# A conformer block on one core: token tiles of 128 rows in place of 127

## The chip, the cores and the metric

The kernel runs on one core of one Trainium2 chip. A core has five engines that run side by side, each with its own queue of instructions: TensorE (PE; its weight loads are listed as PEld), VectorE (DVE), ScalarE (ACT), GpSimd (POOL) and SyncE (SP, which here issues nearly all DMAs). The metric is the device time of one execution in microseconds, the median of three runs.

## What is computed

A conformer block on x of 2 batches x 4000 tokens x 512 features, bfloat16:

```python
h  = silu(layernorm(x) @ w_ff1_a) @ w_ff1_b          # 512 -> 2048 -> 512
x1 = x + 0.5 * h
h  = layernorm(x1)
p  = softmax((h @ w_q) @ (h @ w_k).T * 512**-0.5)    # 4000 x 4000 per batch
x2 = x1 + (p @ (h @ w_v)) @ w_o
a, b = split(layernorm(x2) @ w_pw1)
dc = depthwise_conv3(a * sigmoid(b))                 # 3 taps along the tokens
x3 = x2 + silu(batchnorm(dc)) @ w_pw2
x4 = x3 + 0.5 * (silu(layernorm(x3) @ w_ff2_a) @ w_ff2_b)
out = layernorm(x4)
```

4000 is neither a multiple of 127 nor of 128: 31 x 127 + 63, or 31 x 128 + 32.

## The kernel before

**Tiles and chunks.** Tokens lie on the partitions in tiles of `TILE` = 127 rows (line 16); four tiles make a chunk of `CHUNK` = 508 (line 18). A batch has `TCB` = 8 chunks, seven of 508 and one of 444 (`width`, line 40): three whole tiles and a rest of `TAIL` = 63 rows. The rests of both batches share one tile (`SHARED`), batch 1 from row `HALF` = 64 on (`tile_rows`, line 54), so the 16 chunks hold 63 tiles, and the last chunk of all has three. Half a chunk is `HC` = 254.

**Feed-forward 1** (`ff1`, line 2572) goes through the 16 chunks. In each, 16 blocks of 128 hidden features are made from the transposed, normalised tokens `lnT`, in which every tile has 128 columns per feature group, of which `0:TILE` are read: the moving operand of the first product is 4 pieces of 127 columns (`ff_first`, line 1200), or 2 pieces in the fast chunks, where `ff_quad` (line 1359) forms products of halves so that seven stand for eight. The second product (`ff_units`, line 1244, seven for eight as well) has `TILE` tokens as its weights (stationary) and 256 columns of `Wb` as moving operand. `ff_plain` and `ff_last` do the last chunk, with 381 columns.

**Attention** (`attention`, line 1969). Per chunk of queries, scores against 31 key tiles of 128 and a rest of 32 keys. `q_group` (line 1565) makes the queries `qT`, whose four rows of a partition are `CHUNK` elements long and lie end to end (line 687). The first chunk of a batch multiplies plainly (`scores`, line 1659, moving operand `qT[:, cc, 0:W]`); the other seven do quads of key tiles by seven products of half width (`score_quad`, line 1912), on parts of `qT` and on differences of them, `QF` (line 672). Exponentials go to the buffers `T`, `R` and sums of them `F` (lines 591 to 596, rows of `HC`), which `pv` (line 1757) multiplies with the values, again with seven products for eight. In a quad, product 5 goes to bank h and ACT copies it away; product 1 goes to another bank and ACT copies it into h; product 6 adds to h; DVE's `plus` reads h; only then product 7 may write h.

**Convolution, feed-forward 2.** The pointwise product, gate and taps run beside attention for 13 chunks and after it for the last ones (from line 2682); `G` holds a chunk and a token on either side, in rows of `GW` = 512 elements (line 716). `swish` (line 2439) makes `z`, then feed-forward 2 goes like 1. At the change of stage the weights are loaded in eight slices; `clear` (line 2754) says how many may be loaded ahead of the last convolution work, since the buffers of that work lie in the same place.

**Moves.** A move of token rows goes in two DMAs, rows 0 to 111 and 112 to 126 (`ROWS`, line 532): to and from the copy `xd` in memory (`put_x`, `get_x`), inputs and outputs and the stored keys (`pieces`, line 1004), and the very first tiles (`load_rows`, line 990), where SP issues the first piece and, for two of the four tiles, ACT the second, in the same queue as the first weights.

**Order.** Every operation is first collected and then laid out by `Plan` (line 110): from an estimate of each duration, which depends on the number of elements, it fixes the order of the instructions on each engine. `ff1`, `attention` and the rest only give the order in which operations are offered, how far one may be taken ahead, and the dependences through buffers.

Of the kernel before, what the change touches and what calls it, by code (L numbers as in the profile page):

```python
# [5 lines left out]
F32 = mybir.dt.float32  # L6
# [6 lines left out]
B, T, D, F, KW = 2, 4000, 512, 2048, 3  # L13


TILE = 127
TPC = 4
CHUNK = TPC * TILE
N = B * T
TCB = -(-T // CHUNK)  # L20
FC = F // 128
NCK = B * TCB
TAIL = T % TILE
NT = NCK * TPC - 1
SHARED = TCB * TPC - 1
HALF = 64
PAIRS = 15
GROUPS = 8
QUADS = 7
# [3 lines left out]
DC = D // 128  # L33
# [6 lines left out]
def width(c):  # L40

    return CHUNK if c % TCB < TCB - 1 else T - (TCB - 1) * CHUNK
# [11 lines left out]
def tile_rows(c, ti):  # L54

    if c % TCB < TCB - 1 or ti < TPC - 1:
        return slice(0, TILE)
    lo = c // TCB * HALF
    return slice(lo, lo + TAIL)
# [466 lines left out]
class Conformer:  # L526
# [2 lines left out]
    TAIL_AT = 22  # L529
    NP = 8  # L530

    ROWS = ((0, 112), (112, TILE))

    NBESIDE = 13

# [22 lines left out]
    def memory(self):  # L558
# [5 lines left out]
        self.place(TCB - 1, self.SLOTS)  # L564
        self.xd = nc.dram_tensor("xd", [NCK, TILE, TPC * D], BF16, kind="Internal").ap()
        self.b_xd = [Buf("xd%d" % c) for c in range(NCK)]

        E = Region(nc, "sums", 35840)
# [36 lines left out]
        A = Region(nc, "keys", 65536)  # L605
# [21 lines left out]
        W = Region(nc, "wff", 32768)  # L627
# [11 lines left out]
        def take(n):  # L639
# [6 lines left out]
                    for s in range(2)]  # L646
# [1 line left out]
                      for s in range(2)]  # L648

        self.lins = [[C.view(oLT + s * 4096, DC * n).rearrange("p (c k) -> p c k", c=DC) for s in range(2)]  # L650
                     for n in (512, 448)]
        self.lin = self.lins[0][1]
        oLM = take(4096)
        self.ltm = [C.view(oLM + j * 1024, D) for j in range(TPC)]
# [58 lines left out]
        self.b_ptail = W.buf("ptail", 31744, 2 * CHUNK)  # L713
        self.pqd = nc.dram_tensor("pqd", [128, TILE], BF16, kind="Internal").ap()
        self.b_pqd = Buf("pqd")
        GW = CHUNK + 4
        self.vst, self.b_vst = W.view(28672, 2 * D), W.buf("vst", 28672, 4 * D)
        self.vs2, self.b_vs2 = W.view(30720, 2 * HD), W.buf("vs2", 30720, 4 * HD)
        self.vs1, self.b_vs1 = C.view(oP + 7680, HD), C.buf("vs1", oP + 7680, 2 * HD)
# [4 lines left out]
        self.b_asb = [W.buf("asb", 8192 + k * 2048, 4 * CHUNK) for k in range(3)]  # L724
        self.tmp = W.view(12288, CHUNK, F32)
        self.b_tmp = W.buf("tmp", 12288, 4 * CHUNK)
        self.bst = W.view(14848, DC * NCK * 6, F32).rearrange("p (c t s) -> p c t s", c=DC, t=NCK)
        self.b_bst = [W.buf("bst", 14848 + cc * NCK * 24, NCK * 24) for cc in range(DC)]
        gof = [16384, 20480]
        self.G = [W.view(o, DC * GW).rearrange("p (c k) -> p c k", c=DC) for o in gof]  # L730
        self.b_G = [[W.buf("G", o + cc * 2 * GW, 2 * GW) for cc in range(DC)] for o in gof]
        self.b_Gl = [[Buf("Gl") for cc in range(DC)] for o in gof]
# [41 lines left out]
            st.units = []  # L774
            self.ff.append(st)

        self.two = A.view(65536 - 256, 128)
        self.b_two = A.buf("two", 65536 - 256, 256)

        ns = self.LN_SLOTS  # L780

# [222 lines left out]
    def pieces(self, c, flat, tiles, lo=0, hi=TPC):  # L1004
# [8 lines left out]
        if last:  # L1013
            for b in range(B):
                e = (b + 1) * T
                res.append((flat[e - TAIL:e, :], tiles[b * HALF:b * HALF + TAIL, TPC - 1, :]))
        return res
# [558 lines left out]
    def queries(self, qc, sl):  # L1576

        last = qc == TCB - 1
        return self.lins[last][sl], T - width(qc) - (T - 448) if last else 0

    def fetch_queries(self, b, qc, ti):
        if ti:
# [856 lines left out]
    def swish(self, t, cc):  # L2439
        z, W = self.z[t % 2][:, cc, :], width(t)  # L2440
        parts = [(z[:, 0:W], t, 0, W)]
        if t == TCB - 1:

            parts.append((z[:, W:CHUNK], NCK - 1, 2 * W - CHUNK, W))
        for out, u, lo, hi in parts:
            self.act(out, self.dcv[u][cc][:, lo:hi], AF.Silu,
                     [self.b_dcv[u][cc], self.b_rsc[cc], self.b_shc[cc]], [self.b_z[t % 2][cc]],
                     bias=self.shc[:, cc:cc + 1], scale=self.rsc[:, cc:cc + 1])
# [52 lines left out]
    def constants(self):  # L2501
        S = self.S
        S.op("POOL", lambda e: e.memset(self.neghalf, -0.5), writes=[self.b_neghalf])
        S.op("DVE", lambda e: e.memset(self.zero, 0.0), writes=[self.b_zero])
        for sl in range(self.LN_SLOTS):
            S.op("DVE", lambda e, sl=sl: e.memset(self.st[sl][:, :, 6:8], 0.0), writes=self.b_st[sl])
            S.op("DVE", lambda e, sl=sl: e.memset(self.st[sl][:, :, 8:9], D * EPS), writes=self.b_st[sl])
        for j in range(TPC):
            S.op("DVE", lambda e, j=j: e.memset(self.ltm[j], 0.0), writes=[self.b_ltm[j]])
        S.op("POOL", lambda e: e.memset(self.onef, 1.0), writes=[self.b_onef])  # L2510
        S.op("POOL", lambda e: e.memset(self.eps2, 2 * EPS), writes=[self.b_eps2])
        S.op("DVE", lambda e: e.memset(self.XT[SHARED][HALF - 32:HALF], 0.0), writes=[self.bx[SHARED]])
        S.op("POOL", lambda e: e.memset(self.ident, 0.0), writes=[self.b_ident])
        S.op("POOL", lambda e: e.affine_select(
            out=self.ident, in_=self.ident, pattern=[[-1, 128]], compare_op=ALU.not_equal, fill=1.0,
            base=0, channel_multiplier=1), reads=[self.b_ident], writes=[self.b_ident])
        S.op("POOL", lambda e: e.memset(self.onec, 1.0), writes=[self.b_onec])
        S.op("POOL", lambda e: e.memset(self.one3, 1.0), writes=[self.b_one3])


    def program(self, any_score):
        i = self.i
        self.any_score = any_score
        S = self.S
# [135 lines left out]
        last = NCK - 1  # L2660
# [90 lines left out]
        self.swish(0, 0)  # L2751
        self.swish(0, 1)
        copy_away()
        clear = (14848 - 12288) // (F // self.NWA * 2)
        for k in range(clear):
            self.load_wa(i["w_ff2_a"], k)
        all_t = range(TPC)
# [145 lines left out]
```

## Time and profile before

| what | us |
|---|---|
| median of three runs | 1890.38 (1889.82 to 1892.54) |
| the profiled execution | 1891.78 |
| its span, first to last instruction | 1887.7 |
| PE busy | 1864.2 |
| PEld busy | 1503.1 |
| DVE busy | 1575.4 |
| ACT busy | 1181.0 |
| POOL busy | 133.3 |

Stages by time in the span: feed-forward 1 up to about 400 us, attention to 1412, the change of stage to 1444, feed-forward 2 to the end. Busy times overlap, since the engines run at once. All work stands under line 93, a helper that records every operation, so groups of instructions are told apart by the tiles that they write and read (`y<-work,keys`: into bank y, from the regions work and keys) and by shape: `128*127 128x256` is a matmul with weights of 128 rows and 127 columns and 256 moving columns. `keys`, `sums`, `work`, `wff` and `xt` are the five memory regions, `s` and `y` the eight accumulator banks.

### The profile page before, as it was taken

The page shows a single profiled execution, that of the slowest core. Times are in us where ns is not written, and L with a number is a line of the kernel's source. Part 1 is how long each engine was busy: PE and PEld are TensorE (multiplying, and loading weights), DVE is VectorE, ACT ScalarE, POOL GpSimd, SP SyncE. Part 2 cuts the span into 40 slices and gives each one's busy share as a digit, 9 for nine tenths or more (in the row PEclk, how much of TensorE's full clock was granted, in tenths as well). Part 3 has the DMA queues.
Part 4 walks back from the last instruction along what each step waited for, and adds up shares of the span by engine and source line. Part 5 has one row for each costly group of instructions (what it writes and reads, how often), then busy time and mean ns, then how long its engine had stood idle before and what let it go on. Part 6 is the DMA issues. An engine that isn't in the chain of part 4 may idle for free.

```text
span 1887.7 us, 38980 instructions
## 1 busy us (share of the span) xinstructions
PE 1864.2 (99%) x15362; PEld 1503.1 (80%) x15362; DVE 1575.4 (83%) x3315; ACT 1181.0 (63%) x2061; POOL 133.3 (7%) x235
## 2 busy tenths in 40 slices
PE   9999999999999999999999999999998999999998
PEld 5899999966777777777677777777774999899897
DVE  7788888868779888888888788879887888888875
ACT  5777777644555665565446555655557777777773
POOL 1000000000000000000000000000011000000000
PEclk9999999999999999999999999999999999999999
DMA  8333344297655665447954544454376322322121
GB/s 187 97 85 90 79 112 105 57 259 218 175 145 140 161 189 150 109 134 172 241 128 126 140 120 111 129 137 120 107 208 169 77 57 68 78 46 62 49 43 33
DMA packets 333646, 231.82 MB, mean 123 GB/s; under 512 B 208264, under 2 KB 305867, under 8 KB 333199
## 3 DMA queue, kind: packets, MB, share of 16 engines
q1 hardware_dynamic: 332777, 228.91, 46.7%
q8 instruction: 123, 2.02, 0.5%
q14 instruction: 68, 0.56, 0.1%
q10 hardware_dynamic: 678, 0.34, 0.1%
HBM read 128.30 MB, written 55.65 MB: 97 GB/s over the span
## 4 chain that ended last, share of the span: by engine, by line
PE 93%; DVE 3%; ACT 1%; DMA 1%; issue 0%; SPq 0%; POOL 0%; ACTq 0%; DVEq 0%
PE s L93 47%; PE y L93 46%; DVE work L93 2%; ACT work L93 1%; DMA work<-work 1%; DVE sums L93 1%; DVE xt L93 0%; DVE s L93 0%; DMA wff<-keysd 0%; ACT sums L93 0%; DVE wff L93 0%; SPq L93 0%; DMA xt<-in_x_dram 0%; POOL work L93 0%; ACT xt L93 0%
## 5 line engine op out<-in xcount | busy, mean ns | idle before, releaser
L93 ACT ACTIVATE sums<-s 128x508 bf16<-128x508 f32 (+2 forms) x494 | 288.8, 585 | 262.7 <-PE s L93 261.4
L93 ACT ACTIVATE keys<-s 128x508 bf16<-128x508 f32 (+1 forms) x281 | 164.1, 586 | 189.1 <-PE s L93 168.8
L93 PE MATMUL y<-work,keys 128*127 128x256 bf16 x1920 | 244.7, 273 | 0.0
L93 DVE TENSOR_TENSOR sums<-sums 128x508 bf16<-128x508 bf16 (+4 forms) x528 | 195.2, 398 | 47.3 <-ACT sums L93 43.0
L93 PE MATMUL s<-work,keys 128*128 128x254 bf16 (+5 forms) x1456 | 224.6, 291 | 0.8 <-ACT sums L93 0.6
L93 PEld LDWEIGHTS y<-work,keys 128*127 128x127 bf16 x1920 | 216.2, 137 | 5.1
L93 PE MATMUL y<-wff,keys 128*127 128x256 bf16 (+3 forms) x1592 | 209.1, 276 | 1.1 <-DVE keys L93 0.9
L93 DVE BATCH_NORM_STATS2 work<-xt 127x6 f32<-127x512 bf16 x311 | 204.9, 681 | 5.4 <-DMA xt<-in_x_dram 4.1
L93 PE MATMUL y<-sums,keys 128*128 128x254 bf16 (+1 forms) x1440 | 201.5, 269 | 0.0
L93 PE MATMUL s<-sums 128*128 128x254 bf16 x1296 | 194.3, 273 | 0.0
L93 PEld LDWEIGHTS y<-wff,keys 128*127 128x127 bf16 (+1 forms) x1592 | 176.0, 136 | 15.1 <-issue 3.3
L93 DVE TENSOR_TENSOR keys<-keys 128x1016 bf16<-128x1016 bf16 (+2 forms) x262 | 168.2, 660 | 22.1 <-ACT keys L93 14.1
L93 PE MATMUL y<-work,wff 128*128 128x254 bf16 (+2 forms) x1116 | 184.0, 292 | 0.0
L93 POOL TENSOR_TENSOR work<-work 127x4 f32<-127x4 f32 (+3 forms) x94 | 90.7, 966 | 1111.9 <-DVE work L93 1111.5
L93 ACT ACTIVATE work<-xt,work 127x512 bf16<-127x512 bf16 x204 | 162.0, 807 | 9.6 <-DVE work L93 9.6
L93 PEld LDWEIGHTS y<-sums,keys 128*128 128x128 bf16 x1440 | 139.1, 97 | 23.2 <-issue 0.2
L93 PEld LDWEIGHTS s<-work,keys 128*128 128x128 bf16 (+1 forms) x1456 | 118.8, 97 | 48.5 <-issue 3.4
L93 DVE TENSOR_TENSOR work<-work,sums 128x508 f32<-128x508 f32 (+1 forms) x224 | 150.6, 672 | 2.2
L93 PE MATMUL s<-work,wff 128*128 128x508 bf16 (+4 forms) x660 | 139.9, 348 | 3.6 <-DVE work L93 2.8
L93 PE MATMUL y<-sums,xt 128*128 128x254 bf16 (+1 forms) x960 | 142.7, 269 | 0.3 <-DVE sums L93 0.2
L93 PEld LDWEIGHTS s<-sums 128*128 128x128 bf16 x1296 | 126.7, 98 | 18.1
L93 PE MATMUL s<-work 128*127 128x512 bf16 (+2 forms) x541 | 137.0, 383 | 1.8 <-DVE work L93 1.2
(133 smaller groups left out, 3156.7 us busy)
## 6 DMA issues: line engine op xcount, KB each, us to landing
xt<-kfd SPq DMA_DIRECT2D x98, 384.0 KB, 3.3
xt<-v12d SPq DMA_DIRECT2D x105, 256.0 KB, 3.0
xd<-xt SPq DMA_DIRECT2D x28, 448.0 KB, 3.3
xt<-xd SPq DMA_DIRECT2D x28, 448.0 KB, 4.4
out_dram<-xt SPq DMA_DIRECT2D x14, 448.0 KB, 3.3
dcvd<-wff SPq DMA_DIRECT2D x48, 127.0 KB, 2.3
keys<-dcvd SPq DMA_DIRECT2D x12, 508.0 KB, 4.4
xt<-in_x_dram SPq DMA_DIRECT2D x13, 448.0 KB, 4.1
```

Source lines behind the costliest of these rows:

```text
L93: return getattr(eng, self.name)(*self.args, **self.kw)
```

## The change

The tile becomes 128 rows. With it `CHUNK` is 512, `HC` 256, a batch's eighth chunk 416 wide, `TAIL` 32; the shared tile holds 2 x 32 rows, and `HALF` is 32. A move of rows is one piece, so the first tiles are loaded by SP alone. The query fetch has the chunk's own width (512 or 416 in place of 512 or 448), and `swish` passes on 32 columns in place of 64. Since the buffers are longer, `G` has rows of 514, `bst` and `G` start 256 bytes earlier, and the small matrix `two` lies in another region.

```diff
-TILE = 127
+TILE = 128
-HALF = 64
+HALF = 32
-    ROWS = ((0, 112), (112, TILE))
+    ROWS = ((0, TILE),)
-                     for n in (512, 448)]
+                     for n in (CHUNK, T - (TCB - 1) * CHUNK)]
-        GW = CHUNK + 4
+        GW = CHUNK + 2
-        self.bst = W.view(14848, DC * NCK * 6, F32).rearrange("p (c t s) -> p c t s", c=DC, t=NCK)
-        self.b_bst = [W.buf("bst", 14848 + cc * NCK * 24, NCK * 24) for cc in range(DC)]
-        gof = [16384, 20480]
+        self.bst = W.view(14592, DC * NCK * 6, F32).rearrange("p (c t s) -> p c t s", c=DC, t=NCK)
+        self.b_bst = [W.buf("bst", 14592 + cc * NCK * 24, NCK * 24) for cc in range(DC)]
+        gof = [16128, 20240]
-        self.two = A.view(65536 - 256, 128)
-        self.b_two = A.buf("two", 65536 - 256, 256)
+        self.two = E.view(35840 - 256, 128)
+        self.b_two = E.buf("two", 35840 - 256, 256)
-        return self.lins[last][sl], T - width(qc) - (T - 448) if last else 0
+        return self.lins[last][sl], 0
-            parts.append((z[:, W:CHUNK], NCK - 1, 2 * W - CHUNK, W))
+            parts.append((z[:, W:W + TAIL], NCK - 1, W - TAIL, W))
-        S.op("DVE", lambda e: e.memset(self.XT[SHARED][HALF - 32:HALF], 0.0), writes=[self.bx[SHARED]])
+        S.op("DVE", lambda e: e.memset(self.XT[SHARED][2 * HALF:], 0.0), writes=[self.bx[SHARED]])
-        clear = (14848 - 12288) // (F // self.NWA * 2)
+        clear = (14592 - 12288) // (F // self.NWA * 2)
```

## The prediction

> **What bounds the kernel now.** I read the page first (busy times, chain of work), then the busy times of stretches, then the order of time for TensorE alone, to get the spacing of its matmuls.
>
> ```profile
> span 1887.7 us, 38980 instructions
> PE 1864.2 (99%) x15362; PEld 1503.1 (80%) x15362; DVE 1575.4 (83%) x3315; ACT 1181.0 (63%) x2061; POOL 133.3 (7%) x235
> ...
> PE 93%; DVE 3%; ACT 1%; DMA 1%; issue 0%; SPq 0%; POOL 0%; ACTq 0%; DVEq 0%
> ```
>
> TensorE is busy for 99% of the span and is 93% of the chain that ended last. The stretches (columns: length, PE, PEld, DVE, ACT, POOL, clock, DMA) say where it is not:
>
> ```profile
> 0.00:12.00 12.00, 9.73 (x77) 5.34 (x78) 6.61 (x27) 3.28 (x5) 3.24 (x15) 1.00 0.89 220
> 400.00:1412.00 1012.00, 1003.71 (x8098) 747.67 (x8096) 852.14 (x1811) 562.26 (x989) 59.12 (x134) 1.00 0.57 152
> 1372.00:1396.00 24.00, 21.75 (x212) 17.48 (x209) 18.72 (x43) 15.42 (x30) 1.92 (x5) 1.00 0.80 208
> 1412.00:1444.00 32.00, 26.50 (x146) 13.92 (x143) 23.64 (x57) 24.51 (x40) 8.59 (x26) 1.00 0.62 186
> 1444.00:1870.00 426.00, 425.75 (x3593) 378.64 (x3594) 352.65 (x716) 308.32 (x534) 29.97 (x29) 1.00 0.26 62
> ```
>
> In the second feed-forward TensorE has no gap (425.75 of 426 us), in attention 8 us of 1012; the gaps lie in the head, the last query chunk (1372 to 1396) and the change of stage at 1412. The clock is 1.00. So a change of tile width is priced by one thing: how far apart the starts of consecutive matmuls lie, by width. A mean duration of a matmul (273 ns) is latency and no price; the spacing is the start of the next group minus a group's own start, over its count.
>
> ```profile
> 13.21 7.93 PE L93 MATMUL s<-work,wff 128*128 128x508 bf16 x36
> 20.98 0.72 PE L93 MATMUL y<-work 127*128 127x127 bf16 x10
> ...
> 404.81 2.75 PE L93 MATMUL y<-wff,work 128*127 128x512 bf16 x12
> 407.40 0.81 PE L93 MATMUL y<-wff,sums 128*127 128x512 bf16 x3
> 408.05 3.59 PE L93 MATMUL s<-work 128*128 128x508 bf16 x16
> 411.48 1.46 PE L93 MATMUL y<-wff,sums 128*127 128x512 bf16 x6
> ...
> 386.80 1.46 PE L93 MATMUL s<-work,wff 128*128 128x381 bf16 x8
> 388.10 1.04 PE L93 MATMUL y<-work,keys 128*127 128x256 bf16 x8
> ...
> 452.51 5.32 PE L93 MATMUL s<-work,keys 128*128 128x508 bf16 x24
> 457.67 0.59 PE L93 MATMUL y<-sums,xt 128*128 128x254 bf16 x4
> ...
> 1398.68 3.02 PE L93 MATMUL y<-sums,keys 128*128 128x222 bf16 x30
> 1401.55 1.11 PE L93 MATMUL y<-sums,work 128*128 128x222 bf16 x10
> ```
>
> 512 columns: 2.59 us / 12 = 215.8 ns. 508 columns in one piece, rows 1024 bytes apart (`q_group`): 3.43 / 16 = 214.4. But 508 columns as four pieces of 127 (the first feed-forward product reads `lnT[:, 0:n, cc, 0:TILE]`): 7.77 / 36 = 215.8, as for 512. Three pieces of 127: 1.30 / 8 = 162.5. **An odd piece of 127 already costs what 128 costs.** In the fast chunks 254 columns are two such pieces, mixed half and half with 256-column products:
>
> ```profile
> 110.00:190.00 80.00, 80.00 (x735) 1.00 0.35 88
> ```
>
> 80 us / 735 = 108.8 ns, 109.1 without the two that began before the stretch; over all starts of either kind I get 109.2 (products of 2 x 127) and 109.2 (256). From 256 at 109.2 and 512 at 215.8 a column costs 0.416 ns and an instruction 2.6: 254 in one piece should take 108.3, 222 95.0, 444 187.4, 208 89.2, 416 175.8, 508 214.1.
>
> In attention the pieces are whole, but start at odd places. `qT` has rows of 1016 bytes, `QF` and the sums rows of 508. The plain scores (452.51) take 5.16 / 24 = 215.0, not 214.1; by starts, every second one takes 217 or 218 and the others 213. For 254:
>
> ```profile
> 561.97 0.61 PE L93 MATMUL s<-xt 128*128 128x254 bf16 x4
> 562.42 0.59 PE L93 MATMUL s<-work,keys 128*128 128x254 bf16 x4
> 562.85 0.38 PE L93 MATMUL s<-sums,keys 128*128 128x254 bf16 x2
> ```
>
> Four in 0.45 us (112.5 each), then four in 0.43 (107.5). The first are products on `QF`, where every second operand starts 508 bytes in: those take 111 to 113. Over the ten forms below, waits left out, the mean is 109.1.
>
> **The change, part by part.**
>
> *Feed-forward columns.* 254, 508 and 381 become 256, 512 and 384, all in pieces of 128: 0 us, as the pad was paid. Bounds: 0, or the full line (next part). The second products keep 256 and 512 moving columns; only their weights widen.
>
> *Weight loads.*
> ```profile
> L93 PEld LDWEIGHTS y<-work,keys 128*127 128x127 bf16 x1920 | 216.2, 137 | 5.1
> L93 PEld LDWEIGHTS s<-sums 128*128 128x128 bf16 x1296 | 126.7, 98 | 18.1
> ```
> A load of 128 columns takes 98 ns, of 127 137. Some 3,450 such loads get 39 ns shorter, 135 us of PEld busy time. It is worth 0 us: they lie under matmuls whose spacing is the same 109.2 whichever load stands before. If that cover did not hold, the gain would show as a spacing under 109.2, which no row has for 256.
>
> *Attention columns.* Seven chunks of a batch widen from 508 to 512 queries, the eighth shrinks from 444 to 416; 4000 stay 4000.
> ```profile
> L93 PE MATMUL y<-sums,keys 128*128 128x254 bf16 x1260 | 178.8, 271 | 0.0
> L93 PE MATMUL y<-sums,keys 128*128 128x222 bf16 x180 | 22.7, 257 | 0.0
> L93 PE MATMUL s<-work,keys 128*128 128x508 bf16 x392 | 97.8, 377 | 0.8 <-ACT sums L93 0.6 <-ACT work L93 0.2
> L93 PE MATMUL s<-work 128*128 128x444 bf16 x32 | 7.1, 351 | 0.0
> ```
> These are the largest of each width. Of 254 in one piece ten forms hold 5,404 matmuls: 109.1 to 109.2, +0.4 us. Of 508, 650: 215.0 to 215.8, +0.5. Of 222, 828: 95.5 (2.87 / 30 = 95.7 above) to 89.2, -5.2. Of 444, 100: 187.4 to 175.8, -1.2. Sum **-5.5**. All rows now start on multiples of 512 bytes, as in the 256- and 512-column rows that give the line. Were the late starts to stay, 254 would cost 0.8 more: 5,404 x 0.8 = 4.3, and 508 0.9 more, 0.6: sum -0.6.
>
> *The short chunk.* There TensorE waits for a chain of ACT and DVE:
> ```profile
> 1379.14 0.54 PE L93 MATMUL s<-work,keys 128*128 128x222 bf16 x4
> 1380.10 0.56 PE L93 MATMUL s<-xt,keys 128*128 128x222 bf16 x4 [0.41 <-DVE s L93]
> ```
> 0.96 us between starts that need 0.38: product 7 waits until `plus` has read bank h. In batch 1 PE has only 21.75 us in 24, so not all that it saves is time. DVE's 444 columns become 416 too (about 1 ns each, 620 ns now), so the chain shrinks by 5%, PE by 6. Of the 3.2 us that this chunk saves I count 0.5 as lost; bounds 0 and 3.2. The shared tile's piece of 63 columns (32 matmuls) becomes 32: between 0 and 32 x 31 x 0.416 ns = -0.4; I take -0.2.
>
> *One piece per move.* 97 second DMAs of 15 rows go (28 to `xd`, 28 back, 14 out, 13 in, 14 to the keys). A DMA holds SP for some 0.45 us (2.74 / 6 below), so SP's queue gets about 44 us shorter. No wait is added anywhere. Nobody gains but the head: TensorE's waits name DVE and ACT, never a DMA. In the head it is on the path:
> ```profile
> 0.74 2.74 SPq L93 DMA_DIRECT2D xt<-in_x_dram  x6
> 0.74 0.45 ACTq L93 DMA_DIRECT2D wff<-in_w_ff_a_dram  x1
> 1.23 0.76 ACTq L93 DMA_DIRECT2D xt<-in_x_dram  x1
> 5.03 1.29 DVE L93 BATCH_NORM_STATS2 work<-xt 127x6 f32<-127x512 bf16 x2 [2.18 <-DMA xt<-in_x_dram]
> 7.55 0.40 PE L93 MATMUL y<-work 127*128 127x127 bf16 x4 [0.69 <-DVE work L93]
> ```
> The first tile's last 15 rows are issued by ACT behind a weight load at 1.23 and land 3.8 us later; in one piece they leave from SP at 0.74 and land near 4.2. The chain behind moves up by 0.8, until the 13 warm-up matmuls hold it (PE's last ended 0.69 before 7.55, at 6.86): -0.7, bounds 0 and -0.9.
>
> *Vector work.* 128 x 508 operations grow by 2 to 4 ns. In attention DVE has 852 of 1012 us and gains some 4: covered by 160 idle us. ACT likewise.
>
> *Helper buffers, query fetch, swish.* `two` moves to where `Vs` lies, read last before 1412 and needed at 1877; `bst` and `G` close up, so one weight slice fewer (4, not 5) is loaded early; slice 4 is needed at block 8, 32 matmuls of 215.8 ns = 6.9 us after 1444.25:
> ```profile
> 1431.78 1.28 SPq L93 DMA_DIRECT2D wff<-in_w_ff_a_dram  x1
> 1444.25 6.20 PE L93 MATMUL s<-work,wff 128*128 128x508 bf16 x28 [1.49 <-DVE work L93]
> ```
> Even behind the first late slice (1431.8) plus one more issue and several us of flight it lands before 1451. On SP nothing more urgent queues behind it. `G`'s rows become 1028 bytes, 33 conv matmuls may start badly at 4 ns: 0.1 us. All 0.
>
> **Sum:** -5.5 + 0.5 - 0.2 - 0.7 = -5.9 us. The profiled execution took 1891.78 us, 4.1 beyond its span; it would be 1885.9. That execution is 1.4 above the median of the runs (1890.38), so the forecast for a median is **1884.5**.
>
> **The rivals.**
>
> *Odd spacings stay (1889.4).* If the 111-to-113 starts come from operands that meet in a memory and not from where they begin, attention gives -0.6 in place of -5.5: 1884.5 + 4.9. For: I see starts, not addresses; a `qT` product with 254 columns at 1016 bytes takes 108 all the same. Against: those above 110 sit at the same two places of four in `s<-xt`, 168 times of 168.
>
> *Every column is paid (1893.4).* By the line, from the one-piece row (508 at 214.4): 3,024 products of 2 x 127 go up 0.8, 624 of 508 1.7, 160 of 381 1.2: +3.7; attention by the line -0.4; the rest -0.4: +2.9. Against: the 36 products at 215.8.
> The Trainium skill, "TensorE: Matmul & The Clock Gate", section "Back-to-back issue gap", gives N / 2.4 + 2.5 ns for N columns and speaks for this rival: an estimate of 214.2 for 508 columns. By that rule the trace agrees for one piece (214.4) and for 512 (215.8), but not for four pieces of 127 (215.8): the measurement decides.
>
> *A new order opens waits (slower).* The order of each engine is planned from the sizes, so all of it is laid out anew. The wait at 1380.10 stands in 14 of the 98 score quads:
> ```profile
> PEld s L93 <- DVE s L93: 7.1, 14, 0.8
> ```
> 0.5 us each. Where the planner puts no value products between products 6 and 7, a quad of a full chunk waits as these do. From 20 more of the 84 others on (+10 us) the kernel is slower than 1894.2; 23 give 1896. For: the cover of a quad is whatever the plan puts there, and 14 had too little. Against: all sizes move by the same 0.8%, so little reason to plan otherwise.
>
> *A better order* could as well take away 4 us or more of attention's 8 us of gaps: under 1881.
>
> **How the numbers follow.** The forecast 0.50, odd spacings stay 0.17, every column paid 0.08, new waits 0.17, better order 0.08. About 0.2%, 3.8 us, is what a measurement tells from no change: faster means under 1886.6, slower over 1894.2. The forecast's own bounds (head 0.7 worse or 0.2 better, short chunk 2.7 worse or 0.5 better, both with a little for the order) are 1882 to 1888, of which 0.08 lies over 1886.6. Faster: 0.42 + 0.08 = 0.50; same: 0.08 + 0.17 + 0.08 = 0.33; slower: 0.17. The range goes from 1881 to 1895: it takes in both middle rivals and leaves out most of the new waits and half of the better order.
>
> **What would show it.** Right: products of 2 x 128 at 109.2 and of 4 x 128 at 215.8 in the feed-forward, whose stretch keeps its length within 1 us; only one heap of spacings for 256 in `s<-xt`, near 109; 208 columns near 89; weight loads of 98 ns throughout and no time from it; the first statistics on DVE near 4.2, the first transpose on PE near 6.9. Wrong: a feed-forward longer by 3 us (columns paid); two heaps, 109 and 113 (odd spacings stay); PE's gaps between 400 and 1412 well over 8 us (order), or waits for a DMA there.

## The result and the profile after

| kernel | median | runs | range |
|---|---|---|---|
| before | 1892.55 us | 20 | 1888.93 to 1895.12 |
| after | 1889.16 us | 20 | 1886.17 to 1890.44 |

The ratio is 0.9983 (95%: 0.9976 to 0.9990): 3.2 us less (1.9 to 4.5). The forecast said 5.9 less, and 1884.5 us. Of the 4.7 us between forecast and median, 2.2 are the level (the median of three that the forecast started from, 1890.38, lay that much below the median of twenty), and some 2.5 are the change itself. The profiled execution took 1886.77 us, 5.0 less than that of before; only one other run of the twenty was as short.

The page of the kernel after, span, busy times and shares of the chain:

```profile
span 1882.5 us, 38836 instructions
PE 1859.6 (99%) x15362; PEld 1442.7 (77%) x15362; DVE 1570.6 (83%) x3315; ACT 1180.4 (63%) x2061; POOL 129.9 (7%) x235
...
PE 93%; DVE 3%; ACT 1%; DMA 1%; issue 0%; POOL 0%; SPq 0%; DVEq 0%; ACTq 0%
```

TensorE still bounds the kernel. The same stretches as before (length, PE, PEld, DVE, ACT, POOL, clock, DMA):

```profile
0.00:12.00 12.00, 9.77 (x93) 6.04 (x93) 6.70 (x27) 3.97 (x7) 3.25 (x15) 1.00 0.89 251
400.00:1412.00 1012.00, 1002.37 (x8113) 739.08 (x8111) 849.70 (x1817) 562.47 (x995) 57.86 (x142) 1.00 0.55 153
1412.00:1444.00 32.00, 26.54 (x140) 12.41 (x140) 21.91 (x54) 23.48 (x39) 7.28 (x18) 1.00 0.61 197
1444.00:1870.00 426.00, 425.87 (x3595) 351.46 (x3593) 353.40 (x717) 309.12 (x534) 29.14 (x29) 1.00 0.22 58
```

The count of matmuls shows the gain: 93 for 77 in the first 12 us (the head begins earlier), 8113 for 8098 in attention. In the second feed-forward 3595 for 3593 in the same 426 us: nothing. Weight loads are 27 us less busy there, and nobody is faster for it.

The head of the kernel after, in order of time:

```profile
0.74 1.82 SPq L93 DMA_DIRECT2D xt<-in_x_dram  x4
3.28 0.69 DVE L93 BATCH_NORM_STATS2 work<-xt 128x6 f32<-128x512 bf16 x1 [0.41 <-DMA xt<-in_x_dram]
6.39 0.40 PE L93 MATMUL y<-work 128*128 128x128 bf16 x4 [0.58 <-DVE work L93]
```

Four DMAs for six, the first statistics at 3.28 (5.03 before), the first transpose at 6.39 (7.55).

The spacings of attention, TensorE alone:

```profile
558.15 0.60 PE L93 MATMUL s<-xt 128*128 128x256 bf16 x4
558.59 0.60 PE L93 MATMUL s<-work,keys 128*128 128x256 bf16 x4
559.02 0.60 PE L93 MATMUL y<-sums,xt 128*128 128x256 bf16 x4
...
1394.79 2.85 PE L93 MATMUL y<-sums,keys 128*128 128x208 bf16 x30
1397.47 2.75 PE L93 MATMUL y<-sums,work 128*128 128x208 bf16 x29
```

0.44 and 0.43 us for four of 256 columns, the forms on `QF` (`s<-xt`) no longer dearer than the others; over all starts there is one heap, at 109 and 110 ns, beside some 125 short waits at 117 to 120, most of them in `s<-xt`. 208 columns: 2.68 / 30 = 89.3.

I added up the spacings over all matmuls of both traces, each up to 14 ns above the line (0.416 ns a column and 2.6 a matmul) as price and what lies beyond as wait. Prices: -3.9 us, of which 222 to 208 -5.0, 444 to 416 -1.2, 254 to 256 **+1.5**, 508 to 512 +0.9, the shared tile -0.1. Waits: head and first feed-forward -2.0 (one wait of 0.9 us at 288 is gone by chance, see below), attention +0.3, change of stage and second feed-forward +1.1; from TensorE's last start to the end -0.7. Together -5.2, the difference of the spans. (The span goes from the first to the last instruction; in every execution of either kernel the time is 3.8 to 4.5 us longer.)

### The profile page after: what moved, and what is told of

The parts are those of the page before. It is cut to its first block, busy times and chain, and to the rows that moved or that the text cites. A ratio compares the mean times of both kernels' runs of the same rounds, so it can differ in the third digit from the quotient of the medians.

```text
span 1882.5 us, 38836 instructions
## 1 busy us (share of the span) xinstructions
PE 1859.6 (99%) x15362; PEld 1442.7 (77%) x15362; DVE 1570.6 (83%) x3315; ACT 1180.4 (63%) x2061; POOL 129.9 (7%) x235
## 4 chain that ended last, share of the span: by engine, by line
PE 93%; DVE 3%; ACT 1%; DMA 1%; issue 0%; POOL 0%; SPq 0%; DVEq 0%; ACTq 0%
PE y L93 47%; PE s L93 47%; DVE work L93 1%; ACT work L93 1%; DVE xt L93 1%; DMA work<-work 1%; DVE s L93 0%; DVE sums L93 0%; DVE wff L93 0%; ACT sums L93 0%; DMA vhd<-wff 0%; DMA xt<-in_x_dram 0%; DMA wff<-keysd 0%; ACT xt L93 0%; ACT keys L93 0%
## 5 line engine op out<-in xcount | busy, mean ns | idle before, releaser
L93 ACT ACTIVATE sums<-s 128x512 bf16<-128x512 f32 (+2 forms) x494 | 289.0, 586 | 262.4 <-PE s L93 261.6
L93 PE MATMUL y<-work,keys 128*128 128x256 bf16 x1920 | 244.7, 273 | 0.0
L93 DVE TENSOR_TENSOR sums<-sums 128x512 bf16<-128x512 bf16 (+3 forms) x528 | 192.4, 396 | 46.8 <-ACT sums L93 44.1
L93 PE MATMUL s<-work,keys 128*128 128x256 bf16 (+5 forms) x1456 | 224.9, 292 | 0.0
L93 DVE BATCH_NORM_STATS2 work<-xt 128x6 f32<-128x512 bf16 x311 | 205.3, 682 | 7.6 <-DMA xt<-in_x_dram 5.6
L93 PE MATMUL y<-wff,keys 128*128 128x256 bf16 (+3 forms) x1592 | 209.0, 276 | 0.1
L93 PEld LDWEIGHTS y<-work,keys 128*128 128x128 bf16 x1920 | 187.9, 98 | 25.2
L93 PE MATMUL y<-sums,keys 128*128 128x256 bf16 (+1 forms) x1440 | 200.9, 270 | 0.0
L93 PE MATMUL s<-sums 128*128 128x256 bf16 x1296 | 194.0, 273 | 0.0
L93 PE MATMUL y<-work,wff 128*128 128x256 bf16 (+2 forms) x1116 | 184.0, 292 | 0.0
```

The lines of the kernel that those rows point to most:

```text
L93: return getattr(eng, self.name)(*self.args, **self.kw)
```

## Experiments

All ratios are to the kernel before on the same chip. Theory: the spacings are prices, set by even column counts and by where an operand starts; the head passes its gain on; the rest of the moves, the order and the weight loads are worth nothing. Rivals: the order or the moves hold the gain; every column is paid; the profiled pair is not typical.

**The parts one at a time**

*e1: the kernel before, each move in one piece.*
```
-    ROWS = ((0, 112), (112, TILE))
+    ROWS = ((0, TILE),)
```


> The kernel before with 127-row tiles, but every move of rows in one piece. Theory: the one-piece moves are worth the head (0.5 to 1.2 us: first statistics on DVE near 3.3 to 4.2 us in place of 5.0) and the last store (0.5 us or so), so 1 to 2 us in all; attention's stretch keeps its length within 1 us. Rival (all that the change brought came from the columns of attention): under 0.5 us. Rival (shorter SP queue helps attention too): 3 us or more, with fewer gaps of TensorE between 400 and 1412.

3240.7 us, 1.713 times as long (1.711 to 1.716). Nothing that I had expected. First page lines, then the head:

```profile
span 3236.0 us, 38856 instructions
PE 1996.5 (62%) x15359; PEld 1572.0 (49%) x15362; DVE 1577.8 (49%) x3315; ACT 1181.8 (37%) x2061; POOL 130.8 (4%) x235
```
```profile
9.44 0.69 DVE L93 BATCH_NORM_STATS2 work<-xt 127x6 f32<-127x512 bf16 x1 [6.59 <-DMA xt<-in_x_dram]
14.83 0.69 DVE L93 BATCH_NORM_STATS2 work<-xt 127x6 f32<-127x512 bf16 x1 [4.69 <-DMA xt<-in_x_dram]
20.21 0.69 DVE L93 BATCH_NORM_STATS2 work<-xt 127x6 f32<-127x512 bf16 x1 [4.60 <-DMA xt<-in_x_dram]
```

A tile of 127 rows lands every 5.4 us, about 24 GB/s. So the kernel before could not have had one piece per move; the split into 112 and 15 rows was no ornament, and 128 rows is what makes it unnecessary. Why, e11 shows. Not all of the 1.71 is the loads themselves: with TensorE waiting so often, its granted clock is 0.81 in the mean here.

*e2: the kernel after, each move in two pieces.*
```
-    ROWS = ((0, TILE),)
+    ROWS = ((0, 112), (112, TILE))
```


> The changed kernel with moves of 112 and 16 rows again. Theory: it loses what the one piece gave at the head and the end, 1 to 2 us against the changed kernel, and stays 1.5 to 3 us under the kernel before. Rival (columns alone): as fast as the changed kernel. Rival (pieces alone): as slow as the kernel before.

1889.37 us, ratio 0.9991 (0.9983 to 1.0000). The first transpose is back at 7.72. By its median it is no slower than the kernel after (1889.2, and 1889.3 in e5); by its ratio it is 1.1 to 1.5 us slower. Its interval touches both that of the kernel after and 1: not settled here.

*e3: the kernel before, rows of `qT`, `QF`, sums and factors at multiples of 512 bytes.*
```
-        row = 4 * HC
+        HS = 256
+        row = 4 * HS
...
-        self.qT = [C.view(o, DC * CHUNK).rearrange("p (c k) -> p c k", c=DC) for o in (oQ0, oQ1)]
+        self.qT = [C.view(o, DC * 512).rearrange("p (c k) -> p c k", c=DC) for o in (oQ0, oQ1)]
```


> The kernel before with 127-row tiles and widths of 254 and 508, but qT, QF, T, R and F in rows of 512 and 1024 bytes, so that the operands start at multiples of 512 bytes; the order of TensorE's instructions is the same as before. Theory (late starts cost 4 ns): the heap at 111 to 113 ns goes for 254 columns in s<-xt, and the rest stay at 107 to 108, mean 107.8 in place of 108.9; 5,404 of these and 650 of 508 give 5 to 7 us, so 1885 to 1888: more than the change itself, since 254 even columns are cheaper than 256. Rival (operands meet in a memory, starts do not matter): both heaps stay and the time is that of the kernel before within 1 us.

1889.25 us, ratio 0.9985 (0.9977 to 0.9994): as much as the whole change. By starts, the two heaps of 254 columns (107.5 and 111 to 113) become one at 108 and 109 in all forms but `s<-work,xt` (second halves of `qT` rows, still 508 bytes in), and the prices fall by 2.8 us (the 3.5 in the expectation of g3 still counted three matmuls that this trace lacks). Starts do count.

*e4: the kernel before in the order that is planned from the sizes of the kernel after.*
```
-        return n
+        return {254: 256, 508: 512, 1016: 1024, 127: 128, 381: 384, 222: 208, 444: 416, 888: 832, 111: 104, 63: 32}.get(n, n)
```


> The kernel before with 127-row tiles, its order planned from the sizes of the changed kernel (254 counted as 256, 444 as 416 and so on; a pair of moves as one): 97 of 100 places in TensorE's order are then as in the changed kernel, where 91 are so in the kernel before. Theory (the new order opened waits in the full chunks that took back 1 to 3 us of what the narrower last chunk saves): 0 to 3 us slower than the kernel before, with attention's gaps longer. Rival (the order is worth nothing, the columns were mis-sized): same as the kernel before within 0.5 us. Rival (the order is what made the change faster): 2 us or more faster.

1891.76 us, ratio 1.0001 (0.9993 to 1.0010): no worth of the order by itself shows, and the interval leaves room for 1.3 us less to 1.9 more.

*e5: the kernel after, unchanged.*

> The changed kernel once more, nothing else changed. Theory: the profiled pair showed 5.0 us (1891.78 to 1886.77) only because that execution of the changed kernel began its full clock early (4.54 us; 6.97 us before) and had no disturbed stretch; the columns, the head and the end are worth 3 to 4 us in a typical execution. So the ratio of medians is 0.998 again (0.9975 to 0.9987, -2.5 to -4.7 us), and a second profile lies 1 to 3 us above the first (span 1883.5 to 1885.5). Rival: the gain is the forecast 5.9 us and the first series was unlucky: ratio 0.9969, span 1881 to 1882.5 again.

1889.31 us, ratio 0.9985 (0.9976 to 0.9994), as the first time; span of the profiled execution 1885.4. Its trace follows that of the first within 0.4 us up to 1410 us, then loses 3.0. The windows of that place (columns as above):

```profile
1410.84:1414.25 3.41, 1.43 (x11) 0.76 (x11) 2.80 (x7) 2.30 (x4) 1.36 (x5) 1.00 0.24 95
1414.25:1417.66 3.41, 2.98 (x9) 1.31 (x10) 0.24 (x2) 0.84 (x2) 0.00 (x0) 0.50 0.00 0
1417.66:1438.15 20.49, 18.95 (x96) 8.51 (x94) 13.93 (x35) 17.07 (x29) 5.10 (x12) 1.00 0.64 188
1438.15:1441.56 3.41, 1.64 (x12) 0.88 (x13) 3.41 (x6) 1.52 (x4) 0.00 (x0) 1.00 1.07 391
1441.56:1444.97 3.41, 3.41 (x10) 1.20 (x9) 2.21 (x9) 1.19 (x2) 1.02 (x1) 0.50 0.83 330
```

The granted clock falls to 0.50 for 3.41 us, twice, each time behind 3.41 us in which TensorE had little to do: it waits there for transposes and for the first tile of the second feed-forward. Counting column time only (0.416 ns a column and 2.6 a matmul), those two stretches hold 0.32 and 0.38. In the first profile the poorest such stretch held 0.39, and nothing happened.

*e6 and e7: the kernel after, first feed-forward product of the fast chunks on 127, then 126 of each 128 columns.*
```
-        B = lambda h, k: [self.lnT[s][:, 2 * h:2 * h + 2, 2 * k + j, 0:TILE] for j in range(2)]
+        B = lambda h, k: [self.lnT[s][:, 2 * h:2 * h + 2, 2 * k + j, 0:127] for j in range(2)]
...
-                out = ps[:, u * HC:(u + 1) * HC].rearrange("p (t k) -> p t k", t=2)
+                out = ps[:, u * HC:(u + 1) * HC].rearrange("p (t k) -> p t k", t=2)[:, :, 0:127]
```


> The changed kernel, in which the 3,024 products of 2 x 128 columns of the fast feed-forward chunks (first product) read and write only 127 of each 128 columns: the last token of each tile is left out of them, and one bank is cleared once. Theory (an odd piece of 127 is paid as 128): the spacing of these products stays 109.2 ns and the time that of the changed kernel within 0.5 us (the clearing may cost up to 0.5). Rival (every column is paid, 0.416 ns each): 108.4 ns, 3,024 x 0.83 = 2.5 us less.

> As the run with 127 columns, but 126 of each 128 columns: the last two tokens of each tile are left out. Both theories: four columns fewer a product are paid, 252 columns at 107.5 ns in place of 109.2, 3,024 x 1.67 = 5.0 us less than the changed kernel (4 to 5 in the end, as DVE and ACT still read 512 columns and a few waits come back). What tells them apart is the step: by the theory all 5 us come between 127 and 126, by the rival half of it. A third way: the feed-forward is held by something other than TensorE's columns, then nothing moves.

127: 1892.95 us; 126: 1885.34 us; the kernel after on the same chip 1889.31 (e5). One stretch of the feed-forward from each, 128, 127 and 126 columns:

```profile
110.00:190.00 80.00, 80.00 (x734) 71.49 (x733) 71.85 (x148) 60.84 (x104) 6.06 (x6) 1.00 0.30 87
```
```profile
110.00:190.00 80.00, 80.00 (x732) 71.49 (x731) 71.93 (x148) 60.81 (x104) 6.05 (x6) 1.00 0.31 87
```
```profile
110.00:190.00 80.00, 80.00 (x741) 72.26 (x739) 72.71 (x150) 61.62 (x106) 6.05 (x6) 1.00 0.30 87
```

With 127 TensorE gets through fewer matmuls, not more: those products take 109.9 ns, 0.7 more than with 128, and the time grows by 3.6 us. With 126 they take 107.5, 5.0 us less in all, and the time falls by 4.0. But these two edits also change what lies outside the span: the time exceeds it by 4.8 to 5.6 us in every execution of e6, by 5.5 to 6.0 in e7, and by 3.9 to 4.3 in e5; why is not known. The medians of the spans go from 1885.2 to 1887.8 (+2.6, for 2.5 in prices) and to 1879.8 (-5.4, for -5.0). So an odd piece is paid at least as the next even one, and in the feed-forward a price arrives whole, as far as these few executions can tell. The extra 0.7 need not be the odd piece's own: the kernel before, too, reads 2 x 127 with a column skipped, but writes the two pieces side by side, and pays 109.2; e6 skips a column where it writes, too.

*e8: the kernel after, only the loads of the first four tiles in two pieces.*
```
+            self.ROWS = ((0, 112), (112, TILE))
             self.load_rows(self.XT[ti], self.x_flat[ti * TILE:(ti + 1) * TILE, :], [self.bx[ti]],
...
+            self.ROWS = ((0, TILE),)
```


> The changed kernel, but the loads of the first four tiles are in two pieces again (112 and 16 rows, the second of the first two tiles issued by ACT behind a weight load), all other moves in one piece. Theory: the first transpose goes from 6.4 back to about 7.6 us and everything behind it as well; the time grows by 0.9 to 1.3 us, and the rest of the moves in one piece is worth nothing. Rival (the head is covered by what follows, the first products wait for weights anyway): the first transpose moves, the end doesn't, under 0.3 us.

1891.17 us against 1889.31 on the same chip: 1.9 more, though the first transpose moves by 0.9 only (6.51 to 7.41). The other 1.0 lies outside the span: the time exceeds it by 4.9 to 5.4 us in all executions of e8, and the medians of the spans stand 0.9 apart (1886.1 and 1885.2).

**The clock at the change of stage**

*e9, e10: fillers, in the kernel after and in the one before.* Thirty matmuls whose results are overwritten; two of their six places are shown.
```
+    def fill(self, n, bank, cols, src, b_src):
+        S, (ps, b_ps) = self.S, bank
+        if S.plan:
+            call = Call("matmul", (ps[:, cols], self.ident, src), dict(start=True, stop=True))
+            S.plan.pe[-1].emit.insert(0, lambda: [S.emit_op("PE", call, [self.b_ident] + b_src, [b_ps], False) for _ in range(n)])
...
+        if t == NCK - 1 and jj == 0:
+            self.fill(5, (ps, b_ps), slice(0, 512), self.Wp1[:, 0, 0:512], [self.b_Wp1])
...
+            if c == 0 and f == 0 and cc == 0:
+                self.fill(11, (ps, b_ps), slice(0, 256), self.Wa[:, 0, 0:256], [self.b_Wa[0]])
```


> The changed kernel with 30 matmuls of no use on TensorE at the change of stage (1410 to 1440 us), in front of products that wait there; their results are overwritten, the order of all else is the same. In the second profile of the changed kernel the granted clock was halved from 1414.25 to 1417.66 and from 1441.56 to 1444.97 us, each behind a stretch of 3.41 us in which TensorE had work for less than 0.4 of the time (0.32 and 0.38); in its first profile none was (0.39 the least). Theory: this lottery takes the rest of the gain: 3.2 us in the second profile. With the fillers no such stretch is left: no half clock between 12 and 1880 us, median 1886.5 to 1888 (changed kernel 1889.2), and a narrower spread (2 us, not 4). Rival: the fillers delay the products behind them by what they save, or the clock is halved for another reason: median 1889 or more.

> The kernel before with the same fillers. Theory (the halved clock falls on the changed kernel more often than on the kernel before, whose profile has none): it gains less than the changed kernel, 0 to 1.5 us, and the two filled kernels stand 4 to 5 us apart, as far as the two profiles. Rival (both lose alike, and the two profiles were an odd pair): the filled kernels stand 3 us apart, as the medians of the unfilled ones do.

After, filled: 1887.13 us (1885.99 to 1887.93), ratio 0.9976 (0.9967 to 0.9985). Before, filled: 1890.16 us (1889.73 to 1890.98), ratio 0.9994 (0.9985 to 1.0003). Two windows of the kernel after with fillers:

```profile
1410.84:1414.25 3.41, 3.33 (x26) 1.62 (x24) 3.35 (x9) 2.87 (x5) 1.83 (x7) 1.00 0.77 275
1412.00:1444.00 32.00, 30.20 (x172) 14.55 (x170) 22.94 (x56) 23.37 (x40) 6.99 (x23) 1.00 0.62 201
```

TensorE's 32 us are nearly full, the clock stays at 1.00, and the executions of either kernel spread by 1 to 2 us in place of 4 to 6. So half of the theory holds: the halved clock makes much of the spread (the other filled kernels below spread by up to 3.7). The other half falls: the two filled kernels stand 3.0 us apart, as the rival said. Both kernels lose alike, and the change is worth 3, not 5.

*e12: the kernel before, a second profile.*

> The kernel before, for a second profile of it. Theory: no half clock, or a short one, at the change of stage (its least stretch of 3.41 us was at 0.39, so it can fall either way); span 1886 to 1889. Rival (both kernels lose alike): a half clock there as in the changed kernel's second profile, and a span of 1890 or more.

1891.18 us, span 1886.8. Both expectations half right: one halved stretch, and a span of the usual length:

```profile
1439.16:1442.57 3.41, 1.46 (x16) 0.83 (x13) 3.41 (x9) 1.69 (x4) 0.00 (x0) 1.00 1.08 280
1442.57:1445.98 3.41, 3.41 (x10) 1.19 (x8) 2.28 (x7) 1.19 (x2) 1.02 (x1) 0.50 1.09 305
```

It reached the end of attention 2.5 us ahead of the first profile of before (1411.11 against 1413.62). A wait of TensorE for DVE of 0.7 to 1.1 us, at 215 or 288 us, comes in some executions of either kernel and not in others. So the first profile of before was late by waits, that of after early by the clock, and their difference of 5 was both.

**The price list by itself**

*e11: 24 matmuls of each form and twelve loads, alone.*
```
+ROWS = (128, 127, 126, 125, 121, 120, 113, 112, 96, 64, 63, 15)
...
+    ("c254late", 254, 1, 254, (0, 254), 128),
+    ("p2x127", 127, 2, 128, (0,), 128),
+    ("c255", 255, 1, 255, (0,), 128),
+    ("c256on2", 256, 1, 256, (2,), 128),
+    ("w127c64", 64, 1, 64, (0,), 127),
```


> A kernel of its own that computes nothing of the reference: 24 matmuls each of 26 forms, back to back at full clock, and loads of 128, 127, 126, 125, 121, 120, 113, 112, 96, 64, 63 and 15 rows of 1024 bytes, one after the other. Theory on columns: 4 x 127 costs as 4 x 128 (215.8 ns), 4 x 126 212.5; 2 x 127 109.2 or a little more, 2 x 126 107.5; 508 in one piece 214.2, 255 and 256 109.2; 254 from an even start 108.3, every second one from 508 bytes in 111 to 113; 256 columns from a start 4 to 128 bytes off: 109 or 113, which shows what 'late' means. Weights of 127 columns: as with 128 under 256 moving columns; under 64 moving columns (29 ns) 137 against 98. Rival on starts: the late start costs nothing by itself, the heaps come from operands in one memory; then 254 from 508 bytes in takes 108.3 here. Theory on loads: a count of rows is spread over as many of the 16 transfer engines as divide it (127 and 113 are prime: one engine, some 5 us in place of 2; 128, 112, 96: 16; 126: 14; 125: 5; 121: 11; 120: 15). Rival: odd counts are slow, or only counts above 112.

Six groups of TensorE (digits at the end of a name are left out by the profile):

```profile
74.75 2.79 PE L78 MATMUL ps<-c254late,weights 128*128 128x254 bf16 x24
77.38 2.77 PE L78 MATMUL ps<-c254on,weights 128*128 128x254 bf16 x24
79.99 5.38 PE L78 MATMUL ps<-p2x,weights 128*128 128x254 bf16 x48
...
115.62 1.56 PE L78 MATMUL ps<-w127c,weights 128*127 128x64 bf16 x24
117.01 0.86 PE L78 MATMUL ps<-w128c,weights 128*128 128x64 bf16 x24
117.71 0.60 PE L80 MATMUL ps<-c,weights 128*128 128x512 bf16 x2
```

Every second start 508 bytes in: 2.63 / 24 = 109.6, against 108.3 from an even start (means over the 23 spacings of a group): such a row of even and late starts costs 1.3 per matmul in the mean, not half of the 4 that the late heap shows, as the neighbours are early; with all 24 starts 508 bytes in, the mean is 108.9. 256 columns show the heaps at 4 bytes off and none at 16, 32, 64 or 128. 255 columns take 109.2, as 256; 253 take 108.4, as 254. 2 x 127, here with a column skipped in what is written as well, takes 109.9, 2 x 126 107.6; 4 x 127 216.5, 4 x 126 212.6, 512 215.8. Weights of 127 columns change nothing under 256 moving columns (109.2), cost 3.3 ns under 128 (59.1 for 55.8) and double 64: 1.39 / 24 = 58.0 for 29.2. So the weight loads' 39 ns were free here because 254 and more columns lie over nearly all of them.

The loads (the window of each, 128, 127, 126, 113 rows; the last two columns are DMA share and GB/s):

```profile
0.73:2.92 2.19, 0.00 (x0) 0.00 (x0) 1.77 (x3) 0.00 (x0) 1.00 0.17 60
2.92:10.05 7.13, 0.00 (x0) 0.00 (x0) 6.00 (x8) 0.00 (x0) 1.00 0.06 18
10.05:12.06 2.01, 0.00 (x0) 0.00 (x0) 1.69 (x3) 0.00 (x0) 1.00 0.22 64
19.24:25.75 6.51, 0.00 (x0) 0.00 (x0) 5.48 (x7) 0.00 (x0) 1.00 0.05 18
```

One row fewer, 7.13 us for 2.19; another one fewer, 2.01. 113 rows take 6.51, 125 3.05, 112 1.98. DMA shares of 0.06 and 0.05 are one of sixteen. The Trainium skill, "DMA: Bandwidth & Descriptors", section "Why a DMA increments its semaphore by 16 and not by 1", has the rule: a transfer is spread over the largest number up to 16 that divides its rows, and it gives 127 rows on one engine as an example. The trace agrees: 127 and 113, both prime, go at 18 GB/s.

**The parts again, with fillers**

The spread of 4 us had hidden the parts; with fillers in all of them (and, from here on, on one chip) they can be read better.

*g1: after, first loads in two pieces; g2: all moves in two pieces; h2: all but the first loads in two pieces; h1: the control. g3: before, even starts; g4: before, order of after.* The edits are those of e8, e2, e3 and e4 on top of the fillers; that of h2 sets `ROWS` the other way round from e8.

> The changed kernel with the fillers (1887.1), but the loads of the first four tiles in two pieces again. Theory (the head is passed on whole): first transpose 1.0 to 1.2 us later, and the end too: 1888.1 to 1888.4. Rival (the run without fillers was right at its face, 1.9 us): 1889.0. Third: the head is covered, under 1887.5.

> The changed kernel with the fillers, all moves in two pieces (112 and 16 rows). Theory: nothing beyond the head, so as the run with only the head in two pieces, within 0.4 us. Rival: the 97 DMAs more hold up SP or the transfers somewhere in attention: 1 us or more above it.

> The kernel before with the fillers (1890.2), rows of queries, sums and factors at multiples of 512 bytes, widths and order as before. Theory (the starts are the whole of the columns' gain, 3.5 us by the spacings, of which attention's waits give a part back): 1887.0 to 1887.8. Rival (the gain is in the width, 222 to 208): 1889.5 or more.

> The kernel before with the fillers, in the order that is planned from the sizes of the changed kernel. Theory (order worth nothing): 1890.2 within 0.5. Rival 1 (the new order opens waits, and hides a part of the gain): 1891 or more. Rival 2 (it closes some): 1889.5 or less.

> The changed kernel with the fillers, as the control of the run beside it on the same chip: 1887.1 as before, within 0.6. If it is 1 us higher here, the runs of single parts (head 2.0, all moves 3.2 above 1887.1) had been read against another chip's level, and each of them shrinks by as much.

> The changed kernel with the fillers, the first loads in one piece, all later moves of tiles in two pieces (112 and 16 rows). Theory (the later moves lie beside other work, as the prediction has it): as its control within 0.4 us. Rival (the 97 DMAs more cost something on the path, as the step from the head alone to all moves, 1.2 us, says): 1.0 to 1.4 us above the control.

| with fillers | median | range |
|---|---|---|
| h1: after | 1886.68 us | 1886.23 to 1887.46 |
| g1: first loads in two pieces | 1889.13 | 1887.77 to 1890.31 |
| h2: later moves in two pieces | 1888.91 | 1887.57 to 1890.49 |
| g2: all moves in two pieces | 1890.29 | 1889.04 to 1891.97 |
| g3: before, even starts | 1889.00 | 1886.87 to 1890.60 |
| g4: before, order of after | 1889.53 | 1888.24 to 1890.95 |
| other chip: e9, after | 1887.13 | 1885.99 to 1887.93 |
| other chip: e10, before | 1890.16 | 1889.73 to 1890.98 |

h1 lies 0.45 below e9, so the chips differ by hardly more. One piece per move is worth 3.6 us (g2 to h1). The first loads alone show 2.5, but as in e8 1.0 of it lies outside the span, in every execution of g1 and in none of g2 or h2. By the medians of the spans (1882.6 in h1, 1884.0 in g1, 1884.6 in h2, 1886.0 in g2) the first loads are worth 1.4 and the later moves 2.0, and the two make the 3.4 of all moves. The theories of nothing beyond the head fall with h2. g3 lies between its theory and its rival; g4 is 0.2 under its theory, across chips.

What stands between the kernel before (1890.2) and the changed one in two pieces (1890.3) are the columns, starts and order together. They come out at nothing, but only to within some 2.4 us, as the two ratios are 0.9994 and 0.9992 with 0.0009 either way; without fillers (e2) the same step is 0 to 3.2 us less, and even starts alone bring 2.9 (e3) or 1.2 (g3).

One place where the later moves cost is plain. The loads and statistics of the second chunk, h1, then h2:

```profile
8.33 0.90 SPq L93 DMA_DIRECT2D xt<-in_x_dram  x1
14.72 2.47 DVE L93 BATCH_NORM_STATS2 work<-xt 128x6 f32<-128x512 bf16 x4 [4.24 <-DMA xt<-in_x_dram]
20.24 0.61 PE L93 MATMUL y<-work 128*128 128x128 bf16 x8
```
```profile
7.98 1.40 SPq L93 DMA_DIRECT2D xt<-in_x_dram  x2
16.12 2.47 DVE L93 BATCH_NORM_STATS2 work<-xt 128x6 f32<-128x512 bf16 x4 [5.46 <-DMA xt<-in_x_dram]
20.91 0.72 PE L93 MATMUL y<-work 128*128 128x128 bf16 x8 [0.70 <-DVE work L93]
```

In two pieces DVE has the rows 1.4 us later, and TensorE waits 0.70 for what DVE makes of them. By 31 us h2 is 0.9 behind h1, and behind e9 as well. Where the rest is lost these traces don't show: further on, e9 and h1, two executions of the same kernel, come to stand 1.8 us apart, as much as is looked for.

## Why the prediction was right and wrong

**Feed-forward columns, 0: right.** 426 us hold 3595 matmuls for 3593; e6, e7 and e11 show the rule by itself. The rival "every column is paid" is out.

**Weight loads, 0: right, for the reason given.** The largest group of the kernel after (busy, mean ns of one, idle before):

```profile
L93 PEld LDWEIGHTS y<-work,keys 128*128 128x128 bf16 x1920 | 187.9, 98 | 25.2
```

98 ns throughout, and no spacing is shorter. e11 shows where the cover ends: somewhere between 256 columns (nothing lost) and 128 (3.3 ns).

**Attention columns, -5.5: the step that failed first; -3.8 by the prices.** The effect is there, but the term of 254 columns was mis-sized. Its base, "Over the ten forms below, waits left out, the mean is 109.1", still held short waits of some 10 ns, and was set against a price of 256 without any, 109.2. Counted alike in both traces (spacings from 100 ns to 14 above the line), the mean goes from 109.1 to 109.4; with 8 as the limit, from 109.0 to 109.2. 254 to 256 then costs 1.5 us and not 0.4, and 508 to 512 0.9 and not 0.5. The narrow chunk was right (-5.0 and -1.2 for -5.2 and -1.2). "Odd spacings stay" is out: the late heaps vanish in e3 with nothing else changed. Its price of a late start, too, was a heap's and not a mean: in e11 the neighbours of late starts get back a part of it.

**The short chunk, +0.5: the right effect, too narrow a place.** I let a price fail to arrive only in the short chunk. Waits above 14 ns in all of attention come to 23.0, 21.6 and 22.3 us in the three traces of before (plain, again, filled) and 23.4, 23.1 and 24.2 in those of after: +1.3, half in the first batch's short chunk (2.2 to 2.8), the rest among the full ones. In e7, in the feed-forward, the whole of a price arrived; in attention, where DVE has 850 of 1012 us, less does. From the last matmul of 381 or 384 columns in feed-forward 1 to the last of 222 or 208 in attention, three traces of before take 1000.0 to 1001.4 us (mean 1000.7), four of after (those three and h1) 998.9 to 1000.0 (999.3): 1.4 us less, where the prices of that stage say 3.5 and the prediction said 5.0. How firm that share is is not settled: even starts gave 2.9 us for 2.8 of prices in e3, but 1.2 with fillers (g3 against e10, on different chips).

**One piece per move, -0.7 and "Nobody gains but the head": wrong, up to -3.6 with fillers.** The head moved as said (statistics at 3.28 for 4.2, transpose at 6.39 for 6.9), and by more; in the span it is worth 0.9 (e8) or 1.4 (g1), near the 0.9 and 1.1 us by which the transposes moved. The failing argument is "TensorE's waits name DVE and ACT, never a DMA": they name the last link. In the second chunk DVE stood between, and DVE's own row names the DMA (h2); that is 0.9 us, and the path of the rest of the 2.0 to 2.2 is not shown. One reserve: each of these kernels has an order planned for its own moves, so this is the price of two pieces with its plan.

**Helper buffers, vector work, query fetch: nothing seen**, as said; no wait of TensorE in the traces after leads there.

**The order: right that it is worth little.** e4: 0.4 us less by the median, at most 1.9 either way; g4 0.6 below e10, across chips. The rivals "new waits" and "better order" are both out at the size that they were given.

**The clock: not in the prediction at all.** It read 1.00 in every stretch of the one profile and was taken as given. With the odd waits of the first profile of before, it made a single pair of profiles say 5 where the kernels differ by 3.

So the sign was right and the gain nearly twice too large. By stage, in the same seven traces, feed-forward 1 ends 1.3 us earlier and attention is 1.4 shorter, which is 2.7 of the measured 3.2. How that divides between columns and moves stays open: the three traces with later moves in two pieces (e2, g2, h2) end feed-forward 1 at 402.3 and take 999.9 for attention, so that there each part has about half; by the medians with fillers the moves have all of it. Either way the columns brought much less than the forecast -5.5 and the moves more than -0.7. The two errors run against each other, and it is luck that the forecast was no further off.

**A version better than both** came from the clock: the kernel after with 30 idle matmuls at the change of stage, 1887.13 and 1886.68 us, ratios to before 0.9976 (0.9967 to 0.9985) and 0.9975 (0.9966 to 0.9985), where the kernel after has 1889.2.

## What to carry to other kernels

A price read from spacings is only a price once the smallest waits are out of it, and it reaches the end only as far as no other engine is close behind: make one cheap run that changes a price alone (126 for 128 columns) and see what share arrives, in the span as well as in the time, as an edit can add a microsecond outside the span. When a wait names an engine, ask what that engine waited for; a DMA off the list of waits can still be two links up. Before explaining a difference of 0.2%, find what makes executions of one kernel differ, and take that away first.

## What the runs showed of the hardware

- At the change of stage, a stretch of 3.41 us in which TensorE had column work for 0.31 to 0.38 of the time was followed by 3.4 or 6.8 us at half clock in all 5 cases (e5 twice, e7, e8, e12); at 0.39 to 0.42 it was not, in 7 cases. Where the limit lies is not shown: the two groups lie within 0.01 of each other, and in the first 10 us a stretch at 0.33 was followed by half clock (e3), four at 0.37 to 0.38 were not (e8, e12, g1, g4). The stretches run on a grid of their own against the kernel's start, so one kernel falls on either side. The Trainium skill, "TensorE: Matmul & The Clock Gate", section "What's actually happening", has this free-running window, of 3413 ns, and names an idle window as what halves the clock; the trace agrees on the length, but a window with work for a third of the time was enough.
- Rows of 1024 bytes that land in one DMA go at 60 GB/s for 128 rows and at 18 for 127 or 113 (e11); a whole kernel that moves 127 rows in one piece takes 1.71 times as long, at a granted clock of 0.81 (e1).
- Moving operands cost by pieces rounded up to even columns (255 columns 109.2 ns as 256, 253 108.4 as 254); rows of matmuls that start 4, 444, 508 or 1016 bytes in, all or every second one, take 0.1 to 1.3 ns more in the mean, those that start 16, 32, 64 or 128 bytes in none (e11).
- With 64 moving columns, weights of 127 columns hold TensorE to one matmul in 58 ns, weights of 128 columns let it start one every 29 (e11).
